# A pre-norm block of windowed attention and a shifted MLP on one core: q/k weights loaded from ScalarE's queue, w3 and w4 loaded in four pieces each, and a new sequence of all operations

## The chip, the cores and the metric

The kernel runs on one core of one Trainium2 chip. The metric is the device time of one launch in microseconds (us). A core has five engines with one list of instructions each: TensorE (PE, matrix products; its weight loads are listed as PEld), VectorE (DVE), ScalarE (ACT), GpSimd (POOL) and SyncE (SP, which here issues DMA transfers only). The engines run side by side and meet at semaphores. TensorE writes its results to eight PSUM banks, and DVE or ACT copy ("evict") them to on-chip memory.

## The reference

With S = 2048 rows, D = 448, F = 1792, 16 heads of 28, a window of W = 8 and a dilation of 2, all in bf16 (`ln` is a layer norm without weights):

```python
qkv = ln(x) @ wqkv                        # q, k, v: [16, S, 28] each
idx = pos[:, None] - 2 * arange(8)        # a row sees itself and 7 rows before it, two apart
logits = einsum("hsd,hswd->hsw", q, k[idx]) * 28 ** -0.5   # -1e9 where idx < 0
o = einsum("hsw,hswd->hsd", softmax(logits), v[idx])
h = x + o @ wo
g = gelu(ln(h) @ w1)                      # [S, D], tanh form
hs = (four column quarters of g, shifted by +1, -1, +2, -2 rows) @ w2
x1 = ln(h) + hs
out = h + x1 + gelu(ln(x1) @ w3) @ w4     # w3: 448 x 1792, w4: 1792 x 448
```

## The kernel before, in words

The 2048 rows are 16 tiles of 128. The first half of the program goes over four strips t of four tiles, each through these phases (the letters are the tags in the source):

- N1: statistics of x and the norm, into `lntm`. A1: transpose to `actT`, then the q and k products (`ps<-actT,arena`); their evictions go to `arena`, where q and k lie. V: the v products, evicted to `vt`, and copied by DMA into `vw`, the layout in which a group of rows sees its window.
- A2: four DVE products of q with the shifted k (`qk_r<-arena`, three of 128x4096 and one of 128x2048), each summed over a head by matmuls with a 0/1 matrix (`ps<-qk_r,zc`). S: the softmax (`mx`, `ls`, `pb`) and the transposes of `pb`. A3: four DVE products that spread the probabilities to a band (`bd_r<-arena,bmask`), and matmuls with `vw`. O: the product with wo, and the residual into `xin`.
- B1: norm of the result and its transpose; M: the product with w1 (`ps<-actT,w_s`), gelu into gT, which lies in `arena`.

The second half goes over five units u of 2, 4, 4, 4 and 2 tiles: B2: the shifted product with w2 (`ps<-w_s,arena`) and statistics; T: norm and transpose; W3: 14 products with w3, each followed by a gelu on ACT into `h3T`; B3: the product with w4 (`ps<-arena,h3T`) and the store. Below, a digit behind a phase is its strip or unit: W30 is W3 of unit 0, B12 is B1 of strip 2, A13 is A1 of strip 3.

A strip or unit is transposed either on PE or by a DMA issued from SP (`actT<-lntm`); the table TURN says which. In this kernel strips 0 and 1 of A1 go by PE, everything else by DMA. Every such DMA transpose waits for all DMAs that stand ahead of it in the sequence with a fixed channel, and those behind it wait for it:

```python
if op.insts[0][0] == "dma_start_transpose":
    op.deps.update(turned + moved)
    turned, moved = [op], []
elif op.is_dma and not callable(op.chan):
    op.deps.update(turned)
    moved.append(op)
```

The source first records all operations (`_Sched.add`, `_Sched.group`) without an order. Then `arrange` takes them in the order of the table ORDER, a list of their numbers. This one list sets the order on all engines and queues, and with it which buffer a tile gets: there are 8 PSUM banks, 3 buffers for the q·k products, 4 for the bands, 2 for normed strips and 4 for transposed ones. OTHER lists the operations that take their second engine, as most PSUM evictions can run on ACT or DVE. Semaphore waits follow from the operations' reads and writes (`_emit_plan`). All operations therefore carry the same line in the profile, L986; L981 is the load of ACT's table for exponentials and logarithms, and a table load at L986 is that for gelu. [...]

Of the kernel before, what the change touches and what calls it, by code (L numbers as in the profile page):

```python
# [48 lines left out]
"""  # L49
OTHER = """  # L50
92 102 187 188 381 493 499 502 505 549 550
"""
FULL = (4,)
FILL = (0, 0, 0, 0)
# [226 lines left out]
def bass_sequential_preLN__sliding_local_dilated__mixer_s_mlp__prompt_kernel(  # L281
# [8 lines left out]
    NF = F // 128  # L290
    PADK = 16
    KW = 80
    KVW = PADK + 512
# [17 lines left out]
    with ExitStack() as es:  # L311
# [5 lines left out]
        bd_r = sb("bd_r", [KW, NBD, 2048], BF16)  # L317
        vt = sb("vt", [128, 2, 4, 512], BF16)
        vw = sb("vw", [KW, 2, 8, 512], BF16)
        bmask = sb("bmask", [KW, 64], BF16)  # L320
# [18 lines left out]
        ls = sb("ls", [128, NSM, 512], F32)  # L339
        zs = mx  # L340
        indj = ls[:, NSM - 1, 0:40].bitcast(BF16).rearrange("p (c h) -> p c h", c=5)
        pb = sb("pb", [128, NSM, NW * KW], BF16)
        ost = qk_r[:, 0, 0:NO * D].rearrange("p (k n) -> p k n", n=D)
        ps = es.enter_context(nc.psum_tensor("ps", [128, 8, 512], F32))

# [9 lines left out]
        def arv(off, parts, n):  # L355
            return AR[0:parts, off:off + n]
# [671 lines left out]
```

## Time and profile before

| | us |
|---|---|
| median of 3 runs (lowest, highest) | 193.64 (192.14, 194.31) |
| span of the profiled execution | 189.9 |
| median less span: what lies around the span | 3.74 |
| PE busy, 2434 matmuls | 178.4 |
| DVE busy | 127.4 |
| ACT busy, with 12 table loads of 1.28 | 126.5 |
| POOL busy | 26.9 |
| from the end of the last matmuls (187.35) to the end of the span | 2.55 |

The profiled execution has no time of its own beside its span. It is therefore set against the median of the runs, and the 3.74 us between them are start and end of a launch, in which no instruction of the program is recorded. [...] One per cent of the time is 1.94 us.

### The profile page before, as it was taken

The page shows a single profiled execution, that of the slowest core. Times are in us where ns is not written, and L with a number is a line of the kernel's source. Part 1 is how long each engine was busy: PE and PEld are TensorE (multiplying, and loading weights), DVE is VectorE, ACT ScalarE, POOL GpSimd, SP SyncE. Part 2 cuts the span into 40 slices and gives each one's busy share as a digit, 9 for nine tenths or more (in the row PEclk, how much of TensorE's full clock was granted, in tenths as well). Part 3 has the DMA queues.
Part 4 walks back from the last instruction along what each step waited for, and adds up shares of the span by engine and source line. Part 5 has one row for each costly group of instructions (what it writes and reads, how often), then busy time and mean ns, then how long its engine had stood idle before and what let it go on. Part 6 is the DMA issues. An engine that isn't in the chain of part 4 may idle for free.

```text
span 189.9 us, 5626 instructions
## 1 busy us (share of the span) xinstructions
PE 178.4 (94%) x2434; PEld 107.5 (57%) x2434; DVE 127.4 (67%) x226; ACT 126.5 (67%) x295; POOL 26.9 (14%) x62
## 2 busy tenths in 40 slices
PE   6799989999988668999999999999999999999994
PEld 2494334545443434486544666666545664699973
DVE  6799999999999999897795337673973024001322
ACT  3569999999998999977698677049167004740330
POOL 2340000000002100202910000008026304000000
DMA  5993065554961553663534200518008202300202
GB/s 138 358 281 85 16 112 128 114 131 102 308 202 28 96 114 93 136 159 88 114 66 85 53 3 0 106 34 183 4 0 91 23 0 77 79 3 0 74 28 73
DMA packets 33217, 17.96 MB, mean 95 GB/s; under 512 B 21944, under 2 KB 32680, under 8 KB 33192
## 3 DMA queue, kind: packets, MB, share of 16 engines
q1 hardware_dynamic: 33192, 17.60, 39.7%
q8 instruction: 19, 0.31, 0.7%
q14 instruction: 6, 0.05, 0.1%
HBM read 7.91 MB, written 1.84 MB: 51 GB/s over the span
## 4 chain that ended last, share of the span: by engine, by line
PE 62%; DVE 17%; ACT 11%; DMA 6%; SPq 1%; issue 1%
PE ps L986 62%; DVE qk_r L986 9%; ACT arena L986 3%; DMA xin<-in_A_x_dram 3%; DMA actT<-lntm 3%; DVE bd_r L986 3%; ACT lntm L986 3%; ACT actT L986 2%; ACT vt L986 2%; DVE lntm L986 1%; DVE mx L986 1%; DVE st L986 1%; SPq L986 1%; ACT xin L986 1%; DVE pb L986 1%
## 5 line engine op out<-in xcount | busy, mean ns | idle before, releaser
L986 PE MATMUL ps<-actT,arena 64*128 64x512 bf16 (+1 forms) x756 | 68.8, 329 | 1.3 <-ACT vt L986 1.0
L986 PEld LDWEIGHTS ps<-actT,arena 64*128 64x128 bf16 x756 | 38.6, 94 | 27.3 <-ACT vt L986 2.6
L986 ACT ACTIVATE h3T<-ps 128x512 bf16<-128x512 f32 (+1 forms) x70 | 31.1, 515 | 33.7 <-PE ps L986 33.0
L986 PE MATMUL ps<-arena,h3T 64*128 64x448 bf16 (+2 forms) x434 | 44.5, 343 | 0.0
L986 PEld LDWEIGHTS ps<-arena,h3T 64*128 64x128 bf16 (+1 forms) x434 | 31.2, 94 | 11.5 <-ACT h3T L986 0.2
L986 DVE SCALAR_TENSOR_TENSOR qk_r<-ps,mrs,arena 128x448 bf16<-128x448 f32 (+1 forms) x17 | 10.6, 652 | 40.3 <-PE ps L986 33.2
L986 ACT ACTIVATE arena<-ps 128x512 bf16<-128x512 f32 (+6 forms) x73 | 32.8, 495 | 5.2 <-PE ps L986 4.6
L986 DVE TENSOR_TENSOR qk_r<-arena 128x4096 bf16<-128x4096 bf16 (+1 forms) x16 | 31.9, 2016 | 0.3 <-ACT arena L986 0.3
L986 POOL TENSOR_TENSOR arena<-arena,xin 128x448 f32<-128x448 f32 x16 | 16.7, 1066 | 43.5 <-DVE lntm L986 43.5
L986 DVE TENSOR_TENSOR bd_r<-arena,bmask 80x2048 bf16<-80x2048 bf16 x16 | 19.1, 1216 | 0.2 <-ACT arena L986 0.2
L986 PE MATMUL ps<-actT,w_s 64*112 64x512 bf16 x112 | 13.6, 378 | 2.2 <-DMA actT<-lntm 2.2
L986 PE MATMUL ps<-wo_s,actT 64*128 64x448 bf16 x128 | 14.8, 350 | 0.8 <-issue 0.5
L986 PE MATMUL ps<-w_s,arena 64*128 64x448 bf16 (+1 forms) x128 | 13.9, 350 | 1.0 <-ACT arena L986 1.0
L986 DVE SCALAR_TENSOR_TENSOR arena<-xin,rs_y,ps 128x448 f32<-128x448 bf16 x16 | 10.3, 676 | 4.0 <-PE ps L986 3.9
L986 PE MATMUL ps<-arena,actT 64*128 64x448 bf16 x112 | 12.5, 350 | 0.1
L986 ACT ACTIVATE lntm<-xin,nm 128x448 bf16<-128x448 bf16 x16 | 10.6, 685 | 2.2 <-DVE nm L986 2.0
L986 ACT ACTIVATE rs_x<-mv,epsilon 128x4 f32<-128x4 f32 (+2 forms) x16 | 4.9, 306 | 10.7 <-DVE mv L986 10.5
L986 ACT ACTIVATE actT<-ps 128x512 bf16<-128x512 f32 (+2 forms) x18 | 10.9, 644 | 1.4 <-PE ps L986 1.2
L986 PEld LDWEIGHTS ps<-actT,w_s 64*112 64x112 bf16 x112 | 7.7, 127 | 7.2 <-ACT arena L986 1.6
L986 PEld LDWEIGHTS ps<-w_s,arena 64*128 64x128 bf16 (+1 forms) x128 | 7.2, 94 | 6.1 <-ACT arena L986 1.1
L986 DVE BATCH_NORM_STATS2 st<-xin 128x6 f32<-128x448 bf16 x16 | 9.1, 616 | 1.7 <-DMA xin<-in_A_x_dram 1.4
L986 PEld LDWEIGHTS ps<-wo_s,actT 64*128 64x128 bf16 x128 | 6.2, 94 | 6.0 <-issue 0.9
(72 smaller groups left out, 156.6 us busy)
## 6 DMA issues: line engine op xcount, KB each, us to landing
arena<-in_B_w_dram SPq DMA_DIRECT2D x2, 896.0 KB, 8.1
out_dram<-qk_r SPq DMA_DIRECT2D x15, 112.0 KB, 1.9
arena<-in_B_w_dram SPq DMA_DIRECT2D x2, 784.0 KB, 5.2
vw<-vt SPq DMA_DIRECT2D x4, 320.0 KB, 5.7
vw<-vt SPq DMA_DIRECT2D x4, 256.0 KB, 3.9
arena<-in_A_wqkv_dram SPq DMA_DIRECT2D x2, 448.0 KB, 4.6
xin<-in_A_x_dram SPq DMA_DIRECT2D x2, 448.0 KB, 8.5
xin<-in_A_x_dram SPq DMA_DIRECT2D x3, 224.0 KB, 6.0
```

The costliest lines, as they stand in the source:

```text
L986: inst = getattr(eng, meth)(**kw)
```

## The change

The weights of q and k (two DMAs of 448 KB) are issued from ACT's queue and no longer from SP's. w3 comes in four DMAs of 448 KB (two column halves of each of two row halves) where it came in two of 896 KB, and w4 in four of 4, 4, 3 and 3 blocks of 128 rows where it came in two of 7. ORDER and OTHER are new. New branches for strips listed in NARROW are added; NARROW is empty, so that none of them records an operation, and only the declared height of `bd_r` and `vw` (128 partitions, of which 80 are used) is different. All other tables (TURN, NORM, STATS, POWER, RESIDUAL) are as before.

```diff
 ORDER = """
-8 9 0 1 39 40 41 42 7 10 12 13 14 15 16 33 17 18 19 29 6 43 5 44 20 21 45 46 30 47 48 31 2 50 51 52 36 53 55 56 62 60
+2 0 3 5 7 1 31 32 34 11 35 8 9 10 33 6 12 13 52 53 57 14 58 59 64 62 15 41 60 42 43 54 65 63 16 55 17 61 66 56 44 45
...
 OTHER = """
-92 102 187 188 381 493 499 502 505 549 550
+92 98 188 189 190 191 219 345 448 507 553
 """
 FULL = (4,)
+NARROW = ()
...
-        bd_r = sb("bd_r", [KW, NBD, 2048], BF16)
+        bd_r = sb("bd_r", [128, NBD, 2048 if wide else 1024], BF16)
...
-        def load_rows(chan, dst, src, lo, n):
+        def load_rows(chan, dst, src, lo, n, eng="sp"):
...
-        load_rows("wqk", wqkv_s[:, :, 0:2 * D], A_wqkv, 0, 2 * D)
+        load_rows("wqk", wqkv_s[:, :, 0:2 * D], A_wqkv, 0, 2 * D, "act")
...
-        load_rows("w3", w3_s, B_w3, 0, F)
+        for q in range(2):
+            load_rows("w3%d" % q, w3_s[:, :, q * 896:q * 896 + 896], B_w3, q * 896, 896)
...
-            for f in range(0, NF, 7):
-                dma("w4%d" % f, w4_s[:, f:f + 7, :], w4_v[:, f:f + 7, :], 128 * 7 * D * 2)
+            for f, n in ((0, 4), (4, 4), (8, 3), (11, 3)):
+                dma("w4%d" % f, w4_s[:, f:f + n, :], w4_v[:, f:f + n, :], 128 * n * D * 2)
```

The number of matmuls (2434) and their forms stay. Fourteen operations change their engine. DVE takes two copies of A10's transposed x and the double one of A11, two norms of B10, an eviction each of A12 and A13, and S2's `pb` (which POOL had); it gives to ACT one copy and one eviction of A10, an eviction of S3, two of A33's and one of T0's two norms. In the new list on SP the transposes of A13 and B10 stand directly behind one another; before, three groups of `vw` copies and the loads of w2 and w3 stood between them. The loads of w1, w2 and the first half of w3 stand ahead of the first DMA transpose, and w4's four pieces stand together with strip 3's `vw` copies behind the transposes of T0 and B11.

**The start, on SP and ACT.** SP's list at the program's start, first before and then after (`arena<-in_A_wqkv_dram` of 128x2x896 are the q/k weights, of 128x2x448 the v weights; `xin` is x):

```order
L986 DMA xin<-in_A_x_dram 128x448 x2
L986 DMA xin<-in_A_x_dram 128x2x448
L986 DMA arena<-in_A_wqkv_dram 128x2x896 x2
L986 DMA xin<-in_A_x_dram 128x2x448 x2
L986 DMA arena<-in_A_wqkv_dram 128x2x448 x2
L986 DMA xin<-in_A_x_dram 128x4x448 x2
```

```order
L1032 DMA xin<-in_A_x_dram 128x448 x2
L1032 DMA xin<-in_A_x_dram 128x2x448 x3
L1032 DMA arena<-in_A_wqkv_dram 128x2x448 x2
L1032 DMA xin<-in_A_x_dram 128x4x448 x2
L1032 DMA wo_s<-in_A_wo_dram 28x4x448 x4
```

The q/k weights have left SP's list, and the two middle loads of x stand in their place. ACT's list at the same place, before and after (`mx<-epsilon` is one small Exp, by which the table is loaded early; `rs_x`, `rs_y` are the reciprocal deviations of the first tiles):

```order
L981 ACT_TABLE_LOAD
L986 ACTIVATE rs_x<-mv,epsilon 128x1
L986 ACTIVATE rs_y<-rs_x 128x1
L986 ACTIVATE rs_x<-mv,epsilon 128x1
L986 ACTIVATE rs_y<-rs_x 128x1
L986 ACTIVATE rs_x<-mv,epsilon 128x2
L986 ACTIVATE rs_y<-rs_x 128x2
L986 ACTIVATE actT<-ps 128x512 x3
L986 ACTIVATE mx<-epsilon 128x1
```

```order
L1027 ACT_TABLE_LOAD
L1032 ACTIVATE mx<-epsilon 128x1
L1032 DMA arena<-in_A_wqkv_dram 128x2x896 x2
L1032 ACTIVATE rs_x<-mv,epsilon 128x1
L1032 ACTIVATE rs_y<-rs_x 128x1
L1032 ACTIVATE rs_x<-mv,epsilon 128x1
L1032 ACTIVATE rs_y<-rs_x 128x1
L1032 ACTIVATE rs_x<-mv,epsilon 128x2
L1032 ACTIVATE rs_y<-rs_x 128x2
```

The two weight loads stand on ACT behind the table load and the small Exp, ahead of the first tiles' deviations.

**VectorE around the norm of unit 0.** DVE's list before, up to T0's two norms (`lntm<-arena,nm`; `st<-xin`, `mv<-st` and `lntm<-xin` are B1 of strip 1, the `qk_r` rows q·k products of strip 3, the `bd_r` rows the bands of strip 2, `arena,mv<-xin,rs_y,ps` the sums of unit 0):

```order
L986 TENSOR_TENSOR bd_r<-arena,bmask 80x2048
L986 TENSOR_SCALAR lntm<-xin,mv,rs_y 128x512 x4
L986 TENSOR_TENSOR bd_r<-arena,bmask 80x2048 x2
L986 TENSOR_TENSOR qk_r<-arena 128x4096
L986 SCALAR_TENSOR_TENSOR arena,mv<-xin,rs_y,ps 128x448 x2
L986 TENSOR_SCALAR nm<-mv 128x2
L986 TENSOR_TENSOR qk_r<-arena 128x4096
L986 TENSOR_TENSOR nmr<-nm,rs_y 128x2
L986 TENSOR_SCALAR lntm<-arena,nm,rs_y 128x512
L986 TENSOR_TENSOR qk_r<-arena 128x2048
L986 TENSOR_SCALAR lntm<-arena,nm,rs_y 128x512
L986 SCALAR_TENSOR_TENSOR xin,mv<-ps,xin 128x448 x2
```

And after, up to the one norm of T0 that DVE keeps (`qk_r` here are products of strip 2, `mx` and `ls` the softmax of strip 2):

```order
L1032 TENSOR_TENSOR qk_r<-arena 128x2048
L1032 TENSOR_TENSOR qk_r<-arena 128x4096
L1032 SCALAR_TENSOR_TENSOR arena,mv<-xin,rs_y,ps 128x448 x2
L1032 TENSOR_SCALAR nm<-mv 128x2
L1032 TENSOR_REDUCE mx<-ps 128x64
L1032 TENSOR_TENSOR ls<-ps,mx 128x512
L1032 BN_STATS st<-xin 128x6 x2
L1032 TENSOR_REDUCE mx<-ls 128x64
L1032 TENSOR_TENSOR nmr<-nm,rs_y 128x2
L1032 BN_AGGR mv<-st 128x2
L1032 BN_STATS st<-xin 128x6
L1032 TENSOR_SCALAR lntm<-arena,nm,rs_y 128x512
```

Four products of strip 3, three bands of strip 2, and four norms and some of the statistics of strip 1's B1 now stand behind T0's norm.

**ScalarE around the last gelus of unit 0.** ACT's list before (`h3T<-ps` are the 14 gelus of W30, `ls` and `mx` the softmax of strip 3, `lntm,mv<-xin,nm` the four squared sums of B12, the L981 row the change to the table of exponentials):

```order
L981 ACT_TABLE_LOAD
L986 ACTIVATE rs_y<-rs_x 128x4
L986 ACTIVATE actT<-ps 128x512 x2
L986 ACT_TABLE_LOAD
L986 ACTIVATE h3T<-ps 128x256 x14
L981 ACT_TABLE_LOAD
L986 ACTIVATE ls<-ls 128x512
L986 ACTIVATE mx<-mx 128x64 x2
L986 ACTIVATE lntm,mv<-xin,nm 128x448 x4
```

And after, where the first ten gelus stand further up (the first `rs_x`, `rs_y` are those of B11, the second of B12):

```order
L1027 ACT_TABLE_LOAD
L1032 ACTIVATE rs_x<-mv,epsilon 128x4
L1032 ACTIVATE rs_y<-rs_x 128x4
L1032 ACTIVATE lntm,mv<-xin,nm 128x448 x2
L1032 ACTIVATE ls<-ls 128x512
L1032 ACTIVATE lntm,mv<-xin,nm 128x448 x2
L1032 ACTIVATE mx<-mx 128x64
L1032 ACTIVATE rs_x<-mv,epsilon 128x4
L1032 ACTIVATE mx<-mx 128x64
L1032 ACTIVATE rs_y<-rs_x 128x4
L1032 ACT_TABLE_LOAD
L1032 ACTIVATE h3T<-ps 128x256 x4
```

The last four gelus of W30 stand behind B12's squared sums, S3's exponentials and a second change of the table; before, they stood ahead of all of these.

More of the change, by code (lines that the diff above doesn't have):

```diff
@@ L292, in bass_sequential_preLN__sliding_local_dilated__mixer_s_mlp__prompt_kernel @@
     KW = 80
+    NK = 48
+    wide = [t for t in range(NST) if t not in NARROW]
     KVW = PADK + 512
@@ L365, in bass_sequential_preLN__sliding_local_dilated__mixer_s_mlp__prompt_kernel @@
         kr = [arv(A_KV + t * KVB + 3 * KVW, 128, 4 * KW).rearrange("p (j n) -> p j n", j=4) for t in range(NST)]
-        pt = [arv(A_KV + t * KVB + 4 * KVW, KW, 1024) for t in range(NST)]
+        pt = [arv(A_KV + t * KVB + 4 * KVW, 64 + NK if t in NARROW else KW, 1024) for t in range(NST)]
         maskrow = arv(A_KV + (NST - 1) * KVB, 1, 512)
@@ L416, in bass_sequential_preLN__sliding_local_dilated__mixer_s_mlp__prompt_kernel @@
         pool("memset", ap=mhalf[:], constant=-0.5)
-        for z in (vt[:].rearrange("p s i (h n) -> p (s i h) n", n=32)[:, :, DH:32], pb[:], wo_s[:]):
+        for z in (vt[:].rearrange("p s i (h n) -> p (s i h) n", n=32)[:, :, DH:32], *([pb[:]] if wide else []), *([pn[:]] if NARROW else []), wo_s[:]):
             dve("memset", ap=z, constant=0.0)
@@ L601, in setup, with parities @@
         def setup():
-            par = ls[0:KW, 0, 128:168].bitcast(BF16).rearrange("p (e j) -> p e j", e=2)
-            pool("memset", ap=par, constant=0.0)
-            pool("affine_select", out=par, in_=par, pattern=[[1, 2], [2, KW // 2]], compare_op=ALU.not_equal, fill=1.0, base=0, channel_multiplier=-1)
-            for e in range(2):
-                dve("tensor_reduce", out=bmask[:].rearrange("p (m e r) -> p m e r", m=4, e=2)[:, :, e, :],
-                    in_=bass.AP(par.tensor, par.offset + e * (KW // 2) + 1, [list(par.ap[0]), [8, 4], [1, NW], [1, 8]]), axis=AX.X, op=ALU.max)
+            def parities(mask, parts, at, n, bases):
+                par = ls[0:parts, 0, at:at + n].bitcast(BF16).rearrange("p (e j) -> p e j", e=2)
+                pool("memset", ap=par, constant=0.0)
+                for base in bases:
+                    pool("affine_select", out=par, in_=par, pattern=[[1, 2], [2, n]], compare_op=ALU.not_equal, fill=1.0, base=base, channel_multiplier=-1)
+                m = (n - NW) // 8
+                for e in range(2):
+                    dve("tensor_reduce", out=mask[:].rearrange("p (m e r) -> p m e r", m=m, e=2)[:, :, e, :],
+                        in_=bass.AP(par.tensor, par.offset + e * n + 1, [list(par.ap[0]), [8, m], [1, NW], [1, 8]]), axis=AX.X, op=ALU.max)
+            if wide:
+                parities(bmask, KW, 128, KW // 2, (0,))
+            if NARROW:
+                parities(nmask, 64 + NK, 128 + KW // 2, NK // 2, (0, 64))
             pool("memset", ap=indj, constant=1.0)
@@ L765, in phase_A2 @@
             act(zs[:, sl, :], zs[:, sl, :], ACT.Exp, scale=-1.0)
-            row = lambda v, off, step: bass.AP(v, off, [[v.shape[1] * v.shape[2], 128], [step, NW], [16, 4], [DIL, NW], [1, DIL]])
-            mult = dict(out=row(pb, sl * NW * KW + DIL, KW + DIL), in0=row(ls, sl * 512, 64),
+            narrow = t in NARROW
+            if narrow:
+                kw, nr = 128, 64 + NK
+                out_p = bass.AP(pn, sl * NW * 128 + DIL, [[NSM * NW * 128, 128], [128 + DIL, NW], [64, 2], [1, 32]])
+            else:
+                kw, nr = KW, KW
+                out_p = bass.AP(pb, sl * NW * KW + DIL, [[NSM * NW * KW, 128], [KW + DIL, NW], [32, 2], [1, 32]])
+            src = pn if narrow else pb
+            mult = dict(out=out_p, in0=bass.AP(ls, sl * 512, [[NSM * 512, 128], [64, NW], [16, 4], [DIL, NW], [1, DIL]]),
                         in1=bass.AP(zs, sl * 64, [[64 * NSM, 128], [8, NW], [2, 4], [0, NW], [1, DIL]]), op=ALU.mult)
@@ L773, in turn @@
                 part = (TOP, BOT)[h]
-                return (h, dict(out=banks[h](lambda v: v[0:KW, 64 * r:64 * r + 64]), lhsT=pb[part, sl, r * KW:(r + 1) * KW], rhs=ident[part, part],
+                return (h, dict(out=banks[h](lambda v: v[0:nr, 64 * r:64 * r + 64]), lhsT=src[part, sl, r * kw:r * kw + nr], rhs=ident[part, part],
                                 start=True, stop=True), 64)
@@ L778, in phase_A2 @@
             for h, b in enumerate(banks):
-                copy(pt[t].rearrange("p (n r) -> p n r", r=NW)[:, 64 * h:64 * h + 64, :], b(lambda v: v[0:KW, :].rearrange("p (r n) -> p n r", r=NW)))
+                copy(pt[t].rearrange("p (n r) -> p n r", r=NW)[:, 64 * h:64 * h + 64, :], b(lambda v: v[0:nr, :].rearrange("p (r n) -> p n r", r=NW)))
         def phase_A3(t):
```

63 lines of the change are left out of this document (45 added, 18 removed), and 56 rows, old and new, of the table ORDER.

## The prediction

> **What bounds the kernel now.** I read the page's busy times, then the windows, then the chain of work that ended last.
>
> ```profile
> span 189.9 us, 5626 instructions
> PE 178.4 (94%) x2434; PEld 107.5 (57%) x2434; DVE 127.4 (67%) x226; ACT 126.5 (67%) x295; POOL 26.9 (14%) x62
> ```
>
> TensorE (PE) is busy for 94% of the span, but this mean hides three stages. The columns of the windows are: stretch, length, busy time and count of PE, weight load, DVE, ACT and POOL, then the granted clock, the DMA share and GB/s.
>
> ```profile
> 0.00:12.35 12.35, 9.60 (x99) 6.08 (x101) 9.68 (x27) 5.72 (x18) 5.13 (x36) 1.00 0.86 269
> 12.35:57.50 45.15, 43.24 (x761) 21.30 (x755) 44.80 (x52) 43.99 (x117) 0.00 (x0) 1.00 0.57 134
> 57.00:76.00 19.00, 14.71 (x208) 7.86 (x210) 18.18 (x31) 17.89 (x40) 1.89 (x3) 1.00 0.39 84
> 88.10:190.00 101.90, 99.16 (x1150) 64.19 (x1144) 45.35 (x96) 49.42 (x104) 17.83 (x21) 1.00 0.25 51
> ```
>
> From 12.35 to 57.5 VectorE (DVE) works 44.80 of 45.15 us and ScalarE (ACT) 43.99: both are full, so a delay of either is not made up. From 57 to 76 PE stands idle for 19.00 − 14.71 = 4.29 us while DVE and ACT stay full. After 88.1 PE is the only full engine, and the granted clock is 1.00 throughout. The chain says the same:
>
> ```profile
> 3.22 6.02 DMA xin<-in_A_x_dram
> ...
> 67.10 5.92 DMA actT<-lntm
> 73.07 35.45 PE ps L986 x583
> 108.60 78.75 PE ps L986 x820
> ```
>
> It starts with the wait for the third load of x, runs through ACT and DVE, and from 73.07 to 187.35 it is PE alone. So the change can win before about 90 us only: the later matmuls are the same in number and form and already dense. What counts is how much matmul work is done when PE becomes the only limit.
>
> **The change part by part. 1, the start.** The rows are from the timeline of the first 30 us, the last line from the view of the two q/k weight loads.
>
> ```profile
> 0.80 1.28 ACT L981 ACT_TABLE_LOAD   x1 [0.80 <-PEq L1013]
> ...
> 2.20 0.98 SPq L986 DMA_DIRECT2D arena<-in_A_wqkv_dram  x2
> ...
> 3.22 1.07 SPq L986 DMA_DIRECT2D xin<-in_A_x_dram  x2
> ...
> 8.22 0.80 PEld L986 LDWEIGHTS ps<-actT,arena 64*128 64x128 bf16 x16 [0.24 <-DVE actT L986]
> ...
> 8.92 0.22 ACT L986 ACTIVATE mx<-epsilon 128x1 f32<-128x1 f32 x1
> ...
> 9.27 2.21 DVE L986 BATCH_NORM_STATS2 st<-xin 128x6 f32<-128x448 bf16 x4 [0.91 <-DMA xin<-in_A_x_dram]
> ```
> ```profile
> DMA to landing us min/median/max: 4.0/4.6/5.3
> ```
>
> ACT issues the weight loads behind its table load and the small Exp, at 0.80 + 1.28 + 0.22 = 2.30 us; SP issued them at 2.20. So the weights start no sooner; x's tiles 4 to 7 do, by 1.02 us (3.22 to 2.20). The two issues (0.98 us) hide on ACT before the first tile's statistics. DVE waited 0.91 us for x at 9.27: the gain lies between 0 and 0.91. I take 0.5, because DVE's list now has the first q·k product ahead of this strip's norms, which needs the weights too. The loss is bounded by sharing: if the 448 KB of x pass ahead of the weights, at the window's 269 GB/s they cost them 1.7 us, and the second half, issued at 2.71 and landed 5.3 later at 8.0, lands at 9.7. The first matmul on it ran at 8.22.
>
> **2, w3 and w4 in pieces.** Four more issues on SP at half of 0.98 us each, while SP mostly waits.
>
> ```profile
> arena<-in_B_w_dram SPq DMA_DIRECT2D x2, 784.0 KB, 5.2
> ```
>
> At 784 KB in 5.2 us (151 GB/s) the w4 pieces and the vw copies between them (2.2 MB, behind the transposes of T0 and B11, estimated at 73.5) take 14.6 us, until 88; the next transpose behind them waits for the statistics of B12 and is ready near 90. Cost zero; if that cover went, each us would delay strip 2's MLP start, which has slack while unit 0 runs. The dead branches for a narrower mask add no instruction; the wider buffers of bd and vw are used as before.
>
> **3, the order on DVE.** Unit 0 of the MLP (T0, W30, B30) moves forward.
>
> ```profile
> 0.00:79.97 79.97, 71.09 (x1134) 37.05 (x1136) 76.12 (x116) 71.03 (x177) 8.07 (x40) 1.00 0.58 143
> ```
> ```profile
> 77.11 0.54 DVE L986 TENSOR_SCALAR lntm<-arena,nm,rs_y 128x512 bf16<-128x512 f32 x1
> ...
> 77.74 2.11 SPq L986 DMA_TRANSPOSE actT<-lntm  x1
> ...
> 81.95 5.19 PE L986 MATMUL ps<-actT,arena 64*128 64x256 bf16 x92
> ...
> 88.06 2.81 PE L986 MATMUL ps<-arena,h3T 64*128 64x448 bf16 x28
> ...
> 90.70 0.92 PE L986 MATMUL ps<-wo_s,actT 64*128 64x448 bf16 x8
> ...
> 91.46 0.73 PE L986 MATMUL ps<-arena,h3T 64*128 64x448 bf16 x6
> ...
> 94.11 0.46 PE L986 MATMUL ps<-ident,pb 64*80 64x64 bf16 x16
> ```
> ```profile
> L986 DVE TENSOR_TENSOR qk_r<-arena 128x4096 bf16<-128x4096 bf16 x12 | 27.1, 2282 | 0.3 <-ACT arena L986 0.3
> ...
> L986 DVE TENSOR_TENSOR bd_r<-arena,bmask 80x2048 bf16<-80x2048 bf16 x16 | 19.1, 1216 | 0.2 <-ACT arena L986 0.2
> ...
> L986 DVE TENSOR_SCALAR lntm<-xin,mv,rs_y 128x512 bf16<-128x512 bf16 x8 | 2.7, 404 | 0.0
> ...
> L986 DVE TENSOR_TENSOR pb<-ls,mx 128x512 bf16<-128x512 f32 x3 | 2.0, 682 | 0.0
> ...
> L986 DVE CAST arena<-ps 128x512 bf16<-128x512 f32 x1 | 0.7, 657 | 0.0
> ...
> L986 DVE COPY actT<-ps 128x512 bf16<-128x512 bf16 x1 | 0.4, 418 | 0.0
> ```
>
> Behind T0's norm now stand four products of strip 3 (3 × 2.28 and a half one of 1.14 = 8.0), three bd products (3.6), and four norms with some statistics of B11 (about 2.6): −14.2. In front come, from ACT and POOL, copies worth four of 0.418, two norms (0.404), two evictions (0.657) and one pb (0.682) = 4.5, of which 3.1 stand ahead of T0; ACT takes back a copy, an eviction and one of T0's norms (1.6). Sum ahead of T0: −14.2 + 3.1 − 1.6 = −12.7; instruction by instruction, with overlaps, −12.0. The norm thus ends near 77.65 − 12.0 = 65.6, the transpose lands 3.5 us later, as the old one did, and W30 starts near 69 instead of 81.95, where PE had its hole. This alone could return up to 4.3 us.
>
> **4, the order on ACT takes it back.** The last four gelus of W30 now stand behind B12's four squared sums, S3's Exp and its two small ones, and a table load; the second part of B30 (28 matmuls) waits for them, and everything behind it on PE.
>
> ```profile
> 0.00:89.20 89.20, 80.33 (x1302) 43.85 (x1302) 83.17 (x133) 78.05 (x194) 9.09 (x41) 1.00 0.58 143
> ```
> ```profile
> L986 ACT ACTIVATE arena<-ps 128x512 bf16<-128x512 f32 x23 | 13.0, 618 | 0.0
> L986 ACT ACTIVATE lntm<-xin,nm 128x448 bf16<-128x448 bf16 x16 | 10.6, 685 | 2.2 <-DVE nm L986 2.0
> ...
> L986 ACT ACTIVATE h3T<-ps 128x256 bf16<-128x256 f32 x28 | 9.0, 385 | 12.4 <-PE ps L986 11.9
> ...
> L986 ACT ACTIVATE ls<-ls 128x512 f32<-128x512 f32 x4 | 2.5, 635 | 0.0
> ...
> L986 ACT ACTIVATE mx<-mx 128x64 f32<-128x64 f32 x8 | 2.0, 253 | 0.8 <-DVE mx L986 0.8
> ```
>
> B12's squared sums wait for DVE's means. DVE had done 76.12 us of work at 79.97, after 3.85 us idle; the new list adds 4.5 − 1.6 = 2.9 moved in and about 1.3 for two residual additions and the means: 80.3 + 3.85 = 84.2. ACT then needs 4 × 0.685 + 0.635 + 2 × 0.253 + about 0.4 (Ln and Exp of the variances) + 1.28 (table) + 4 × 0.385 = 7.1, a little less with overlap: **release at 91.1**. At that point PE will have done, beyond what it had done at 88.06 before, 14 of B30, 8 of the wo product and 16 transposes: by the rows' distances 14 × (90.70 − 88.06)/28 + (91.46 − 90.70) + 0.46 = 2.5. The same work stood done at 88.06 + 2.5 = 90.6, so PE is 0.5 us late, and from there dense.
>
> **Sum**: +0.5 − 0.5 (x) + 0 (pieces) = 0. The profiled span 189.9 and the median 193.64 differ by 3.74 us that lie around the span; I assume them unchanged: 189.9 + 3.74 = 193.6, rounded up to 193.8 because the transposes' bound below lies on the late side only.
>
> The row first: x's loads landed 6.02 us after their issue, behind the 896 KB of weights on the same queue. [...]
>
> **Rivals.** *Faster, ACT is not behind.* By work alone ACT could be free earlier: 78.05 us were done when the last such gelu ended at 89.20; the new list puts 4.1 to 4.3 of B12 and S3 ahead, and gives away a net four evictions' worth (4 × 0.618 = 2.5): 79.8. Idle of 12.35 − 5.72 = 6.63 and 45.15 − 43.99 = 1.16 cannot be avoided: 87.6. Then the release is bound by PE's own work near 88, 2.6 before 90.6; with x 3.1. This needs DVE to deliver the means 3 us sooner than I reckon, by closing its 3.85 us idle. Middle 191.1; full 190.5. For it: PE's hole is filled certainly, so W30's first ten gelus run early. Against it: DVE is full and gets 2.9 us more.
>
> *Slower, the weights share.* The weights land at 9.7 instead of 8.0, the first matmuls are 1.5 late (9.7 − 8.22), DVE's and ACT's full stretch passes it on, and x's 0.5 is not gained: 193.8 + 1.5 to 2.0 = 195.5. It decides as soon as the weights land later than about 8.3. For it: the DMA share of 0.86 in that window.
>
> *Slower, the transposes.* The new list on SP has A13's and B10's transposes directly behind one another, and each waits for the DMAs ahead of it.
>
> ```profile
> DMA to landing us min/median/max: 3.5/4.4/5.9
> ```
>
> At 4.4 the second lands near 48.8 (39.6 + two of 4.4, and a short wait for its norms), just as M0 is due. At 5.9 each it lands at 51.5, and gelus on the full ACT slip by 2.7: 196.5.
>
> *The change doesn't do what it says*: the weights don't start sooner from ACT (2.30 against 2.20); only x moves. That is in the forecast, at no price.
>
> **How the numbers follow.** Forecast 193.8 with 0.38; its own range is 192.5 to 195.2, from the 1.3 us by which the release and x's gain can be off. Faster by ACT 0.31; the weights 0.18; the transposes 0.13. One per cent, 1.9 us, is about what a measurement of this kernel can tell from no change. The middle of the faster rival passes that bound; both slower ones pass it on the whole: chances 0.31, 0.38, 0.31. The range 190.3 to 197.0 takes in all four cases to their bounds and leaves out two of them adding up.
>
> **What would show it.** Weights landing by 8.3 and DVE's wait at 9.27 gone: step 1. W30's first matmul at 68 to 70: step 3. The last of its gelus near 91, waiting for B12's means, and PE's idle moved from 57–76 to just before it: step 4. I am wrong if W30 starts after 75, if PE has holes after 92, or if the full stretch of DVE and ACT starts later than 9.7.

## The result, and the profile after

The changed kernel takes 197.56 us (median of 4 runs, 196.89 to 199.61); the kernel before, measured beside it, 193.27 us. The ratio is **1.030 (95% interval 1.022 to 1.038)**: it is slower, beyond the upper end of the range that was given (197.0). Measured a second time it took 197.22 us, ratio 1.029 (1.024 to 1.033).

The page of the changed kernel: span, busy times, and the row of the granted clock in 40 slices.

```profile
span 195.2 us, 5646 instructions
...
PE 182.8 (94%) x2434; PEld 99.6 (51%) x2434; DVE 130.6 (67%) x228; ACT 125.7 (64%) x294; POOL 26.3 (13%) x61
...
PEclk9979999999999999999999999999999999999999
```

The third slice (9.8 to 14.6 us) has a clock of 0.7. The page of before has no row PEclk: no clock was recorded in that execution, and the 1.00 of its windows, from which the prediction reads a granted clock of 1.00 throughout, measures nothing. The pace of its matmuls has to be read instead. The execution with this span of 195.2 took 196.89 us, so 1.7 us lie around a span. The same holds, within 0.1 us, for every timed execution. The 3.74 us that the prediction put there were thus 2 us too many: the profiled execution of before took about 191.6 us, less than the median and less than each of the four that were timed beside the changed kernel (192.14 to 194.31).

The windows of the changed kernel, in the columns of the prediction, with one stretch more (74 to 96):

```profile
0.00:12.35 12.35, 8.12 (x45) 4.18 (x47) 8.41 (x22) 4.07 (x10) 4.18 (x32) 0.87 0.89 277
12.35:57.50 45.15, 42.22 (x633) 20.76 (x631) 42.17 (x60) 42.39 (x112) 0.98 (x6) 1.00 0.56 124
57.00:76.00 19.00, 17.82 (x324) 8.97 (x324) 18.48 (x32) 18.42 (x45) 2.72 (x3) 1.00 0.43 87
74.00:96.00 22.00, 20.53 (x382) 12.21 (x380) 20.43 (x31) 17.61 (x43) 0.00 (x0) 1.00 0.52 129
96.00:193.00 97.00, 96.57 (x1108) 55.47 (x1104) 43.50 (x90) 45.44 (x91) 18.44 (x21) 1.00 0.22 49
```

and the last new stretch in the kernel before:

```profile
74.00:96.00 22.00, 22.00 (x348) 13.61 (x346) 18.41 (x40) 18.08 (x42) 7.79 (x9) 1.00 0.56 129
```

In the first 12.35 us 45 matmuls ran where 99 had run. PE's idle time between 57 and 76 fell from 4.29 to 1.18 us, as the new order meant it to; but 1.47 us of idle time are new between 74 and 96. From 96 on PE is dense, as before. Of the chain of work that ended last, four pieces:

```profile
1.73 5.34 DMA xin<-in_A_x_dram
7.09 1.15 DVE st L1032 x2
8.80 4.84 PE ps L1032 x52
...
97.32 95.32 PE ps L1032 x1094
```

Before, the chain began with the load of x's tiles 4 and 5 (issued at 3.22; it is x's fourth load, not the third, as the prediction calls it). Now it begins with the load of tiles 2 and 3, which stands one load earlier in x's list, and PE alone ends it from 97.32 instead of 73.07.

**Where the lag arises.** For each trace I added up PE's matmuls without those on a constant at the start (the warm matmuls), each by its columns and by how many of its kind run side by side (in the kernel before, 92 of 64 rows and 256 columns took 5.46 us, 0.06 each, while the last warm ones, of 128 rows and 512 columns, start 0.22 us apart), and asked when the same amount of work was done. The table gives how many us later than before (its 189.9 us trace) that was. It includes two experiments that are told below.

| matmul work done, us | 4 | 10 | 30 | 50 | 55 | 70 | 80 | 160 |
|---|---|---|---|---|---|---|---|---|
| changed kernel | 3.2 | 4.5 | 7.0 | 5.2 | 2.8 | 5.5 | 6.3 | 5.3 |
| changed, weights on SP | −0.1 | 1.2 | 3.7 | 1.7 | −0.7 | 1.9 | 2.8 | 1.8 |
| changed, 17 warm matmuls | 1.8 | 3.1 | 5.6 | 4.0 | 1.5 | 3.0 | 3.8 | 2.8 |

The first two rows are 3.3 to 3.6 us apart from the start to the end: **what the changed kernel loses in the first 13 us is never made up**. The third row, in which PE is at full pace, is 1.9 us behind the second at first and 1.0 at the end, so there a part of the late start does come back. The second row is the sequence alone: it falls back, is 0.7 us ahead after 55 us of work (about 75 us in time), is 2.8 us behind after 80 (some 26 us later) and 1.8 at the end. Each row is one execution; that of the second took 193.35 us, 0.9 us less than its kernel's median.

### The profile page after: what moved, and what is told of

Read it like the earlier page. It is cut to its first block, busy times and chain, and to the rows that moved or that the text cites. A ratio compares the mean times of both kernels' runs of the same rounds, so it can differ in the third digit from the quotient of the medians.

```text
span 195.2 us, 5646 instructions
## 1 busy us (share of the span) xinstructions
PE 182.8 (94%) x2434; PEld 99.6 (51%) x2434; DVE 130.6 (67%) x228; ACT 125.7 (64%) x294; POOL 26.3 (13%) x61
## 4 chain that ended last, share of the span: by engine, by line
PE 73%; ACT 13%; DVE 8%; DMA 3%; issue 2%; SPq 0%
PE ps L1032 73%; ACT arena L1032 7%; DMA xin<-in_A_x_dram 3%; ACT lntm L1032 2%; DVE bd_r L1032 2%; DVE st L1032 2%; DVE qk_r L1032 1%; ACT actT L1032 1%; ACT xin L1032 1%; ACT vt L1032 1%; DVE pb L1032 1%; DVE mx L1032 1%; SPq L1032 0%; ACT rs_x L1032 0%; DVE lntm L1032 0%
## 5 line engine op out<-in xcount | busy, mean ns | idle before, releaser
L1032 PE MATMUL ps<-actT,arena 64*128 64x512 bf16 (+1 forms) x756 | 71.2, 333 | 2.8 <-issue 1.2
L1032 PEld LDWEIGHTS ps<-actT,arena 64*128 64x128 bf16 x756 | 38.1, 95 | 31.4 <-PE ps L1032 2.8
L1032 PE MATMUL ps<-arena,h3T 64*128 64x448 bf16 (+2 forms) x434 | 45.4, 343 | 0.2
L1032 ACT ACTIVATE arena<-ps 128x512 bf16<-128x512 f32 (+6 forms) x73 | 33.6, 490 | 6.9 <-PE ps L1032 5.8
L1032 PEld LDWEIGHTS ps<-arena,h3T 64*128 64x128 bf16 (+1 forms) x434 | 25.0, 94 | 17.6 <-PE ps L1032 0.5
L1032 DVE TENSOR_TENSOR bd_r<-arena,bmask 80x2048 bf16<-80x2048 bf16 x16 | 18.5, 1212 | 0.0
L1032 DVE TENSOR_SCALAR lntm<-arena,mv,rs_y 128x512 bf16<-128x512 f32 x14 | 8.2, 641 | 10.1 <-ACT rs_y L1032 8.7
L1032 PE MATMUL ps<-arena,actT 64*128 64x448 bf16 x112 | 13.1, 350 | 1.1 <-ACT arena L1032 0.7
L1032 PEld LDWEIGHTS ps<-w_s,arena 64*128 64x128 bf16 (+1 forms) x128 | 6.2, 94 | 6.2 <-PE ps L1032 1.0
L1032 PEld LDWEIGHTS ps<-wo_s,actT 64*128 64x128 bf16 x128 | 5.4, 94 | 6.9 <-ACT actT L1032 1.3
```

The costliest lines, as they stand in the source:

```text
L1032: inst = getattr(eng, meth)(**kw)
```

## The start of the changed kernel

The timeline of the changed kernel's first 18 us (start, duration, engine, operation, and in brackets the idle time before it with its releaser; ACTq and SPq are the queues that issue DMAs):

```profile
0.81 2.83 SPq L1032 DMA_DIRECT2D xin<-in_A_x_dram  x5
...
0.94 0.94 ACTq L1032 DMA_DIRECT2D arena<-in_A_wqkv_dram  x2
...
1.63 4.57 PE L1032 MATMUL ps<-ident 128*128 128x512 bf16 x11 [1.63 <-POOL ident L1032]
...
2.10 0.20 ACT L1032 ACTIVATE mx<-epsilon 128x1 f32<-128x1 f32 x1
...
5.24 0.63 DVE L1032 BATCH_NORM_STATS2 st<-xin 128x6 f32<-128x448 bf16 x1 [1.34 <-DMA xin<-in_A_x_dram]
...
7.09 1.15 DVE L1032 BATCH_NORM_STATS2 st<-xin 128x6 f32<-128x448 bf16 x2 [1.01 <-DMA xin<-in_A_x_dram]
...
8.80 1.75 PE L1032 MATMUL ps<-ident,lntm 128*128 128x128 bf16 x16 [2.61 <-DVE lntm L1032]
...
10.48 6.77 PE L1032 MATMUL ps<-actT,arena 64*128 64x256 bf16 x98
```

Three things are to be seen. The weight loads leave ACT's queue at 0.94 us, during the table load and ahead of the small Exp at 2.10, though they stand behind both in ACT's list: here the issue of a DMA that waits for nothing does not wait for ACT's unit. So the first of them is under way before SP has issued x's second load (1.27) and the second before its third (1.73), and these land at 5.2 and 7.07 us, where they had landed at 4.0 and 5.0. And PE, which had nothing to do for 2.61 us, then takes 1.75 us for the sixteen transposes that took 1.42 before, and 6.77 us for 98 matmuls. The same places in the kernel before:

```profile
4.00 0.63 DVE L986 BATCH_NORM_STATS2 st<-xin 128x6 f32<-128x448 bf16 x1 [0.26 <-DMA xin<-in_A_x_dram]
...
5.03 1.15 DVE L986 BATCH_NORM_STATS2 st<-xin 128x6 f32<-128x448 bf16 x2 [0.18 <-DMA xin<-in_A_x_dram]
...
6.73 1.42 PE L986 MATMUL ps<-ident,lntm 128*128 128x128 bf16 x16 [0.97 <-DVE lntm L986]
...
8.25 5.46 PE L986 MATMUL ps<-actT,arena 64*128 64x256 bf16 x92
```

The granted clock of the changed kernel us by us:

```profile
9.00:10.00 1.00, 1.00 (x13) 0.83 (x11) 0.98 (x4) 0.63 (x2) 0.17 (x1) 0.58 1.09 349
10.00:11.00 1.00, 1.00 (x12) 0.69 (x11) 0.57 (x3) 0.60 (x1) 1.00 (x6) 0.50 1.11 341
11.00:12.00 1.00, 1.00 (x14) 0.71 (x12) 1.00 (x4) 0.00 (x0) 1.00 (x7) 0.50 1.14 316
12.00:13.00 1.00, 1.00 (x16) 0.79 (x14) 1.00 (x3) 0.00 (x0) 1.00 (x13) 0.71 1.14 200
```

It stood at half for about 3.4 us (0.84 + 1 + 1 + 0.58 by these rows). The idle stretch ahead of it, with matmuls on both sides, was 2.61 us long.

## The experiments

Each is compared with runs of the kernel before on its own chip; ratios carry a 95% interval. Where an experiment starts from "the changed kernel with the weights on SP", that is the first one below.

**The weights back on SP.**

```diff
-        load_rows("wqk", wqkv_s[:, :, 0:2 * D], A_wqkv, 0, 2 * D, "act")
+        load_rows("wqk", wqkv_s[:, :, 0:2 * D], A_wqkv, 0, 2 * D)
 ORDER: 12 13 (the two loads) behind 10 (x's third load)
```

> The changed kernel, but the q/k weights are issued from SP again, between x's third and fourth load, as before. Theory 'start' (the weights, issued from ACT at 0.94 us, pass x's second and third load, so that the first norms begin at 7.1 instead of 5.0 us; the lag of some 3 us at 20 us stays to the end): first matmul on normed x back at 6.7 us, time 194.2 to 194.9. Theory 'order' (the start's lag is swallowed later, the new sequence costs the 4 us by itself): 196.5 or more. If my forecast of the sequence alone was right, 193.3 to 194.0.

Measured: 194.23 us, ratio 1.012 (1.007 to 1.017). This is 'start': about 3 us of the loss go with this one edit, and the time is inside the range that was given. What stays, 1.2% or 2.3 us, is the new sequence. Its first matmuls on x:

```profile
6.66 1.42 PE L1032 MATMUL ps<-ident,lntm 128*128 128x128 bf16 x16 [0.73 <-DVE lntm L1032]
...
8.06 5.86 PE L1032 MATMUL ps<-actT,arena 64*128 64x256 bf16 x98
```

**More warm matmuls in the changed kernel.** Nothing of x's lateness is touched.

```diff
...
-                keep_busy()
+                keep_busy((), 2 if n >= WARM - 6 else 1)     # the last six issue two matmuls each
```

> The changed kernel with 17 instead of 11 matmuls on a constant at the start, so that PE is busy until about 8.8 us, when the first norm arrives. If the granted clock of 0.87 between 10 and 20 us comes from PE's idle 2.6 us at 6.2 to 8.8 and is passed on: clock 1.00 there and 0.8 to 1.7 us less than the changed kernel, 195.8 to 196.8. If the clock is low for another reason, or ACT and DVE set the pace there anyway: no change, 197.2 to 197.8.

Measured: 194.63 us, ratio 1.014 (1.010 to 1.018), and a granted clock of 1.00 (in two of the ten executions 0.999). That is more than was expected: x is as late as in the changed kernel, and still nearly all of the 3 us come back.

```profile
6.89 1.15 DVE L1032 BATCH_NORM_STATS2 st<-xin 128x6 f32<-128x448 bf16 x2 [0.69 <-DMA xin<-in_A_x_dram]
...
8.59 1.42 PE L1032 MATMUL ps<-ident,lntm 128*128 128x128 bf16 x16 [1.42 <-DVE lntm L1032]
...
9.99 5.21 PE L1032 MATMUL ps<-actT,arena 64*128 64x256 bf16 x86
```

The transposes take 1.42 us again. So the late x costs the changed kernel mostly because PE's pace is halved behind it: by the medians 2.9 of 3.3 us come back, by the three traces 2.5 of 3.5. The rest is work that starts later.

**The slow pace without a late x.** The changed kernel with the weights on SP, with four of the eleven warm matmuls at full length and seven of 64 columns.

```diff
...
-                keep_busy()
+                keep_busy((), n >= 4)                        # small: 64 columns
```

> The changed kernel with the q/k weights on SP, and with only four of the eleven matmuls on a constant at full length (seven of 64 columns), so that PE stands idle for 2.3 to 3 us ahead of the first norm while x arrives as early as before. Theory 'clock' (an idle stretch of that length ahead of the first transposes halves the granted clock for some 3 to 4 us, and the lag stays): clock near 0.5 for 3 us between 6 and 12 us, and a time 1.5 to 3 us above that with eleven, 195.7 to 197.2. If the late x harms and not the clock: 194.0 to 194.8, with or without the low clock.

Measured: 195.77 us, ratio 1.021 (1.016 to 1.025): 0.8% or 1.6 us above the same kernel with eleven, which was measured on another chip; the two intervals just touch. x came in time, and the slow pace alone costs this.

```profile
1.63 2.26 PE L1034 MATMUL ps<-ident 128*128 128x512 bf16 x11 [1.63 <-POOL ident L1034]
...
6.62 1.89 PE L1034 MATMUL ps<-ident,lntm 128*128 128x128 bf16 x16 [2.73 <-DVE lntm L1034]
8.80 7.40 PE L1034 MATMUL ps<-actT,arena 64*128 64x256 bf16 x96 [0.29 <-ACT actT L1034]
```

The expected low clock can't be read here: this page has no row PEclk either, so that its 1.00 is no measurement. The pace shows it, and shows something else than was expected. The four full warm matmuls start 0.43 us apart, which is the slow pace (in the run with 17 the last eight start 0.22 us apart), and the transposes are slow from the first on. PE is at the slow pace in all three rows; that an idle stretch took it away is not shown by this run. The changed kernel's second measurement shows the same pace.

> The changed kernel once more, nothing edited. Low clock in every execution: 196.9 to 199.6 with granted clocks of 0.98 to 0.99, as in its first four; an execution with 1.00 throughout, if there is one, near 194.7, as with seventeen matmuls on a constant.

Measured: 197.22 us (196.32 to 197.84). Four executions are recorded at 0.991 and two, with 197.41 and 197.84, at 1.00; the expected 194.7 for such a one did not come. In the one at 1.00 that was profiled PE was slow for longer than before:

```profile
1.63 4.88 PE L1032 MATMUL ps<-ident 128*128 128x512 bf16 x11 [1.63 <-POOL ident L1032]
8.41 1.89 PE L1032 MATMUL ps<-ident,lntm 128*128 128x128 bf16 x16 [1.91 <-DVE lntm L1032]
10.23 7.68 PE L1032 MATMUL ps<-actT,arena 64*128 64x256 bf16 x98
```

Eleven matmuls in 4.88 us are 0.44 us each; in the run with 17 these took 5.54 us in all, so the later ones ran at twice the pace. The pace never rose here during the warm matmuls. The page of this execution has no row PEclk, and its 1.00 stands where no clock was recorded; the time of a known group of matmuls is the safer reading. So the changed kernel comes to the slow pace in two ways: in the first trace the pace had risen and fell after the 2.61 us of idle time (the first transposes start 0.06 us apart, those after 9.16 us 0.11), in this one it had not risen when the warm matmuls ended, at 6.51. Which of the two the 17 matmuls prevent, they do not tell apart.

**The weights on ACT, but issued where the prediction had them**, behind the small Exp.

```diff
-        act(zs[:, 0, 0:1], epsilon[:, 0:1], ACT.Exp)
-        load_rows("wqk", ..., "act")
+        small = act(zs[:, 0, 0:1], epsilon[:, 0:1], ACT.Exp)
+        load_rows("wqk", ..., "act", [small])                # both loads wait for it
```

> The changed kernel, with the two weight loads on ACT waiting for the small Exp, so that they are issued near 2.3 us, the time I had reckoned with, behind x's first three loads. If only the early issue harms: x's third load lands at 5.0 to 5.5 us, time 194.2 to 195.0, as with the loads on SP. If two queues that share the DMA engines harm as such: x's third load or the weights land 1.5 us or more late (the weights at 9 or later) and the time is 195.5 to 197. Theory 'order': 196.5 or more.

Measured: 195.0 us, ratio 1.013 (1.004 to 1.021), at the upper end of the first expectation and no different from the weights on SP within the intervals. The trace shows the rival of the prediction to the tenth: x is in time, and the weights, issued at 2.33, are waited for until 9.67. Its price is not settled: the two profiled executions (194.93 us here, 193.35 with the weights on SP) are 1.6 us apart, the medians 0.8, the ratios 0.1%, and the interval is 0.9% to either side.

```profile
2.33 0.94 ACTq L1032 DMA_DIRECT2D arena<-in_A_wqkv_dram  x2
...
4.64 1.15 DVE L1032 BATCH_NORM_STATS2 st<-xin 128x6 f32<-128x448 bf16 x2
...
9.67 5.54 PE L1032 MATMUL ps<-actT,arena 64*128 64x256 bf16 x94 [1.90 <-DMA arena<-in_A_wqkv_dram]
```

**The weights on ACT in the kernel before**, and the same with 17 warm matmuls.

```diff
-        load_rows("wqk", wqkv_s[:, :, 0:2 * D], A_wqkv, 0, 2 * D)
+        load_rows("wqk", wqkv_s[:, :, 0:2 * D], A_wqkv, 0, 2 * D, "act")
 ORDER: 2 11 12 13 (constant, small Exp, the two loads) at the front
```

> The kernel before, with nothing changed but the q/k weights, which are issued from ACT behind the small Exp, which moves to the front of ACT's list (with the constant it reads). Theory 'start': x's second load lands near 5.2, the third near 7.1, and the time rises by 2 to 3.5 us, to 195.3 to 196.8. Theory 'order': the old sequence has room for it, 193.0 to 194.2.

> The kernel before with the q/k weights issued from ACT at 0.94 us and with 17 instead of 11 matmuls on a constant at the start. With 11 it was 3 us (1.4%) above before. If that was TensorE's pace after an idle stretch: the matmuls of the first strip at the pace of before, and 192.3 to 193.2. If it was the late x itself: 194.5 to 195.5.

Measured: 195.42 us, ratio 1.014 (1.007 to 1.020), as 'start' expects; and with 17 warm matmuls 194.25 us, 1.012 (1.006 to 1.018), which lies between its two expectations. In the old sequence the move alone costs 1.4%. Its trace shows the slow pace from the first warm matmul on, and that with 17 the full pace:

```profile
1.63 4.87 PE L986 MATMUL ps<-ident 128*128 128x512 bf16 x11 [1.63 <-POOL ident L986]
8.87 1.89 PE L986 MATMUL ps<-ident,lntm 128*128 128x128 bf16 x16 [2.37 <-DVE lntm L986]
```
```profile
8.81 1.42 PE L986 MATMUL ps<-ident,lntm 128*128 128x128 bf16 x16 [1.26 <-DVE lntm L986]
```

Yet the ratios are only 0.2% apart, the medians 1.2 us, on two chips and with intervals of 0.6 to 0.7% to either side. That the pace and not the late x is the larger part is therefore shown for the new sequence only.

**The pieces alone.** The old order and engines, w3 and w4 in four pieces each.

> The order and engines of before, q/k weights on SP, with w3 and w4 in four pieces each, the pieces one behind another where the two halves stood. If the pieces cost nothing, as I reckoned: 192.0 to 192.9 (within 0.3% of before). If four more issues and smaller transfers hold up the transposes behind them: 0.5 us or more above before.

Measured: 191.49 us, ratio 0.997 (0.994 to 1.001). No cost can be seen.

**The old engines in the new sequence.** OTHER of before, in the changed kernel with the weights on SP.

```diff
-92 98 188 189 190 191 219 345 448 507 553
+94 104 189 190 383 495 501 504 507 553 554
```

> The changed kernel with the q/k weights on SP as before, and with the fourteen operations on the engines that they had before; the sequence is the new one. If the 2.9 us that DVE was given ahead of unit 0 are what the new sequence costs: 1.0 to 2.0 us less than with the new engines, so 192.4 to 193.2 (equal to the kernel before within 0.5%). If the place of the last W30 gelus on ACT costs it: no more than 0.5 us less, 193.8 to 194.4, or more, since ACT gets that work back.

Measured: 199.78 us, ratio 1.039 (1.034 to 1.045). Both theories are wrong by a wide margin. Giving DVE 2.9 us of work was no cost of the new sequence: without it the same sequence is 2.7% slower. A stretch at half clock from 21.5 to 24.9 us, behind a wait of PE of 1.90 us, is a part of that in the profiled execution.

**W30's last gelus ahead of B12 and S3.**

```diff
 ORDER, behind 315 (the last gelu of M1):
+578 582 583 579 584 580 581 585          (W30's last four matmul groups and gelus)
 594 595 301 ...                          (B21, B12, S3 as they were)
```

> The changed kernel with the q/k weights on SP; the last four matmul groups of W30 moved ahead of B21's on PE, and its last four gelus on ACT directly behind M1's, ahead of the table change, B12 and S3. Two table loads go. Theory 'release' (B30's second part waits for these gelus behind B12 and S3, released at 92.2 us, and this costs what the sequence loses): release near 88, and 1.0 to 1.8 us less than with the weights on SP alone: 192.4 to 193.2. Theory 'PE does other work meanwhile': within 0.5 us of it, 193.7 to 194.7.

Measured: 198.88 us, ratio 1.037 (1.030 to 1.043). The release did come 2 us sooner (89.96 instead of 92.1), but B12's squared sums and S3's exponentials now stood behind it, and PE waited for S3's probabilities:

```profile
88.70 1.26 ACT L1032 ACTIVATE h3T<-ps 128x256 bf16<-128x256 f32 x4 [3.84 <-PE ps L1032]
```
```profile
92.33 1.49 PE L1032 MATMUL ps<-arena,h3T 64*128 64x448 bf16 x14
96.26 0.74 PE L1032 MATMUL ps<-ident,pb 64*80 64x64 bf16 x16 [2.44 <-DVE pb L1032]
```

**The same, with S3's transposes behind three parts of B30 on PE.**

```diff
 ORDER: 493 494 496 499 495 (S3's transposes and what follows) from ahead of 587 to behind 588
```

> As the run with W30's last gelus ahead, and S3's sixteen transposes (with what follows from them) moved on PE from behind the first to behind the third of B30's four parts, so that PE has 28 matmuls of B30 to do while ACT and DVE finish S3's softmax. If the release of B30 behind B12 and S3 is what the sequence loses: no wait of PE over 1 us between 85 and 100 us and 192.4 to 193.4. If the two chains on ACT (gelus, softmax) only change places, strip 3 is late now: 194.5 to 197.

Measured: 201.76 us, ratio 1.053 (1.049 to 1.057). The wait has moved on once more, to the bands of strip 3:

```profile
95.60 0.46 PE L1032 MATMUL ps<-ident,pb 64*80 64x64 bf16 x16
101.02 0.62 PE L1032 MATMUL ps<-bd_r,vw 80*32 80x64 bf16 x32 [4.95 <-DVE bd_r L1032]
```

In this run and the one before it, the windows behind the wait show the clock at half, for about 6.8 and 3.4 us, so a part of either price is pace.

**Halves of the two sequences.** First the new order for 490 operations and then the rest in the order and on the engines of before; then the old one for 400 and the new one for the rest.

> As the changed kernel with the q/k weights on SP up to and with the first ten gelus of W30 and the residual of strip 2 (490 of its 862 operations), then all that is left in the order and on the engines of before: there W30's last four gelus stand ahead of S3's exponentials and B12's squared sums on ACT, and T1 ahead of B12. Theory 'step 4' (the release of B30 behind B12 and S3 on ACT costs what the filled hole gave): release at 86 to 88 instead of 92 us, and a time of 190.5 to 192.0, faster than the kernel before by 0.4 to 2 us. Theory 'elsewhere' (the loss lies ahead of this point): 193.5 to 194.5.

> The order and engines of before for the first 400 operations (to strip 0's MLP and strip 2's softmax, about 62 us), then all that is left in the new order and on the new engines; q/k weights on SP, w3 and w4 in pieces. If the sequence loses behind that point (W30 to B30): as the changed kernel with the weights on SP, 193.8 to 195. If it loses ahead of it (strips 0 to 2, where its lag was 4 us above that of before at 50 us): 191 to 192.5, faster than both.

Measured: 201.33 us, ratio 1.050 (1.044 to 1.055), and 204.33 us, 1.065 (1.058 to 1.072). Neither says which half costs, since each seam makes waits that neither sequence has (in the first, PE idles 4.48 us for S3's probabilities; in the second 9.79 us for a transpose, up to 81.07).

**The norms of strip 1 ahead of the first product**, as before had them, in the changed kernel with the weights on SP.

```diff
 ORDER: 139 (the first q-k product of strip 0) from ahead of N11's norms to behind 214, the last of them
```

> The changed kernel with the q/k weights on SP; the first q-k product of strip 0 on DVE moved behind the four norms of strip 1, as the kernel before has it. The lag at 10 to 20 us (2.3 us more than before) comes from DVE waiting there for ACT's evictions, if that is so it falls by 0.5 to 1 us there; whether it lasts: if DVE is full up to 80 us, as I reckoned, the end is 0.5 to 1 us earlier, 193.2 to 193.8; if slack further on takes it up, no change, 193.8 to 194.6.

Measured: 196.48 us, ratio 1.022 (1.016 to 1.028): slower by 1%, where either expectation was the same or faster. The lag at 20 us of work rose instead of falling: PE waited 2.10 us for a copy, and behind that wait the clock was at half (0.50 between 22 and 25 us).

```profile
20.00:22.00 2.00, 1.50 (x12) 0.53 (x14) 2.00 (x2) 1.54 (x6) 0.00 (x0) 0.95 0.03 13
22.00:25.00 3.00, 3.00 (x26) 0.65 (x24) 2.32 (x4) 1.77 (x4) 0.00 (x0) 0.50 0.72 197
```

**Filling PE's waits in the kernel before.**

```diff
...
+                    mms([(fill_bank, ident[:, 0:KC], ..., 512, None)] * (7 if t == 0 else 4))   # M0, M1
```

and, in a second kernel, in M0's wait alone:

```diff
+                if g == 2 and t == 0:
+                    mms([(A[0](0, 512), ident[:, 0:KC], ..., 512, None)] * 6)
```

> The kernel before, with matmuls on a constant put into the waits of PE for DMA transposes: seven of 512 columns (1.5 us) ahead of M0 and four (0.9 us) ahead of M1, written to the bank that M0 and M1 then overwrite. If the executions of before with a mean clock of 0.98 to 0.99 lose it at these waits: all at 1.00, median 191.0 to 191.6 against 191.8 to 192.4. If they lose it elsewhere: the same scatter, or slower by what the extra matmuls hold up, up to 1 us.

> The kernel before with six matmuls on a constant (512 columns, 1.3 us) directly ahead of M0's first matmul, inside PE's wait of 1.53 us for M0's transpose. If the clock falls behind this wait in the executions with a mean clock of 0.98 to 0.99: all executions at 1.00 and within 190.4 to 191.6, median 0.5 to 1.2 us below before. If it falls elsewhere: the same scatter as before, within 0.5 us of it.

Measured: 194.97 us, ratio 1.017 (1.012 to 1.022), in a run that tells little, as the extra matmuls came to stand behind M0's first eight matmuls, not in the wait. With six of them in the wait itself: 192.85 us, ratio 1.007 (1.004 to 1.010), and four of twelve executions still with a mean clock below 0.995. So the wait for M0 is not the only place where the kernel before loses its clock. It can be one: in the trace of the weights on ACT in the old sequence the clock fell at 69.0 us, behind a wait for M0 of 1.54 us. No version here beats the kernel before.

## Why the prediction was wrong, step by step

- **What bounds the kernel**: right. DVE and ACT are full to about 80 us, then PE alone, and most of what is lost early stays lost. The clock of 1.00 throughout was read from a trace that has no record of it; PE's pace there is full from the transposes on (1.42 us for the sixteen), so the reading did no harm to this part, but it hid that pace is a price.
- **Step 1, the start**: this failed. It had the weights issued at 2.30 us, behind the table load and the Exp; they were issued at 0.94. It therefore had x's tiles 4 to 7 as what gains (−0.5), and looked for the price of sharing at the weights. The weights won instead, and tiles 1 to 3, the ones everything waits for, came 1.2 and 2.1 us late. It counted PE's start by when work could begin and had no term for the pace at which PE then runs. Measured: 1.2% for the sequence alone, 1.4% with the late x at full pace, 3.0% with the halved pace. The term "−0.5" was about +3.4 us (1.2% to 3.0%). Without it the time, 194.23 us, lies inside the range: this step alone took the result out of it.
- **The rival "the weights share"** was right that one load comes later for another, with the wrong victim and 1.5 to 2 us. Built as it was described, it appeared with its 9.67 us (forecast 9.7). Its price, 1.5 to 2 us, is neither confirmed nor excluded: 0.1% over the weights on SP by the ratios, 1.6 us by the two traces.
- **Step 2, the pieces**: right, 0.997 (0.994 to 1.001).
- **Step 3, T0's norm**: right where the start is undisturbed. With the weights on SP its norm ended at 65.69 us (forecast 65.6):

```profile
65.16 0.53 DVE L1032 TENSOR_SCALAR lntm<-arena,nm,rs_y 128x512 bf16<-128x512 f32 x1
...
90.92 1.21 ACT L1032 ACTIVATE h3T<-ps 128x256 bf16<-128x256 f32 x4
```

  W30 began at 70.5 (near 69), and in the changed kernel everything is 3.5 us later: 68.67 + 0.53, and 74.0. But the step counted the work handed to DVE as a delay only. ACT was as full as DVE, and the run with the old engines shows that in this sequence the handing over is worth 2.7%.
- **Step 4, ACT's order**: the release came at 92.1 (forecast 91.1) with the weights on SP, and at 95.65 in the changed kernel. The two experiments that brought it forward were slower, so the place of these gelus is not shown to be what the sequence loses; they stand where S3 and B12 leave room. Forecast for the sequence +0.5 us, measured 2.3 (1.4 to 3.3). The windows of that run show PE's idle time: 2.01 us instead of 4.29 between 57 and 76, and 1.51 instead of 0 between 74 and 96.

```profile
57.00:76.00 19.00, 16.99 (x320) 8.95 (x318) 18.67 (x31) 18.43 (x47) 2.73 (x3) 1.00 0.31 60
74.00:96.00 22.00, 20.49 (x356) 10.97 (x344) 20.45 (x32) 16.72 (x39) 0.00 (x0) 1.00 0.51 128
```

  The two windows overlap, and 1.15 us stand in both: one wait from 74.82 to 75.97, which the profile puts down to nothing that it shows. From 76 to 96 PE idles 0.36 us only. The hole was filled, then, and yet the table of the lag has the sequence lose 3.5 us between 55 and 80 us of work; what the 1.5 us of idle time do not cover is lost while PE counts as busy. What holds it there stays open: every edit of the sequence that was tried made a new wait of 2 to 10 us.
- **The rival "back-to-back transposes"** did not come: with the weights on SP the two end near 48.7 us, as reckoned at their median (48.8).
- **The sum's base**: 3.74 us around the span were 1.7. The forecast stood on the median, so this did not move it; it means that the trace of before is an execution of about 191.6 us, quicker than those that were timed beside the result.

## What to carry to other kernels

A load moved to a second queue does not only start sooner, others can come later for it, as here x's second and third load by 1.2 and 2.1 us: ask which transfer everything waits for, and whether the moved one can now pass it. An instruction list is no timetable for DMAs: here two that wait for no semaphore were issued at 0.94 us, ahead of the Exp at 2.10 that stands before them. And price a wait of PE at its length plus what follows it: here 2.6 us of idle time near the start were followed by about 3.4 us at half pace, and in the new sequence the lost pace cost more than the wait (2.9 of 3.3 us by the medians). How many matmuls on a constant do at the start is to be tried anew when the first loads move: with x early, eleven were followed by transposes at full pace (1.42 us, the weights on SP), with x late by slow ones (1.75 and 1.89), and 17 by 1.42 again.

## What the runs showed of the hardware that was not expected

- DMAs behind a table load and an Exp in ACT's list were issued at 0.94 us, while the table load ran (0.80 to 2.08); with a semaphore wait on the Exp, at 2.33.
- An idle stretch of PE of 2.61 us between matmuls was followed by about 3.4 us at half clock: sixteen transposes took 1.75 us instead of 1.42, and 98 matmuls 6.77 instead of 5.86. Shorter ones were followed by it too, 2.10 us (the norms ahead, a clock of 0.50 from 22 to 25 us) and 1.90 (the old engines, 0.51 in the same stretch), but not each: a wait of 1.90 us in the run with the waiting weights was followed by 94 matmuls in 5.54 us, as fast as the 98 in 5.86 with the weights on SP.
- Eleven warm matmuls did not always bring PE to full pace. In three traces they took 4.87 or 4.88 us, 0.44 each; in two of these the transposes then took 1.89 us, in the third 1.43.
- A clock of 1.00 does not exclude this where the page has no row PEclk: two such traces have 7.40 and 7.68 us for the first 96 and 98 matmuls.
- The kernel before scatters with the mean clock: beside the last experiment 190.4 to 191.9 us at 1.00, 191.4 to 192.3 at 0.991, 193.9 to 194.3 at 0.982. Where the clock falls there was not found, as none of its traces is of such an execution. The nearest is the pieces alone, with the order and the engines of before: its trace, at 0.982, has the clock at half from 60.0 to 63.4 and from 73.7 to 77.1 us, the first time behind a wait of PE of 2.17 us that the profile puts down to nothing that it shows.
